# Router rows and logits from one float32 product with unit matrix and gate

## The chip, the cores and the metric

The kernel runs on one core of a Trainium2 chip. The metric is the device time in microseconds of the whole program; the median of several runs counts.

## The reference, cut to what matters

Three layers follow one another on 24576 tokens (8 sequences of 3072) of 256 features. The third routes each token to one of 8 experts:

```
X = rfft(x, axis=1); Y = softshrink(X @ (w_r + i w_i) + b, 0.01); x = irfft(Y)      # per sequence
h = x @ w_in                                                                        # 256 -> 2048
g = where(h >= 1, h, where(h <= -1, 0, (h + 1)**2 / 4));  x = g @ w_out             # 2048 -> 256
logits = x @ w_gate                                                                 # 256 -> 8
expert_idx = argmax(logits);  gate_w = softmax(logits)[expert_idx]
out[mask_e] = gate_w * (relu(x[mask_e] @ w1[e]) @ w2[e])                            # 256 -> 1024 -> 256
```

## The kernel before, in words

It has three stages. `spectral` (to about 560 us in the trace) does the transforms as products of 48 by 64 points; `Moe1` (to about 2927 us) is the dense layer; `Moe2` is the expert layer. The order of all instructions is written out by hand, and each engine and each DMA queue works through its own list in that order.

`Moe1.run` goes through 48 units of 512 tokens, 16 steps each. A step multiplies one slice of 128 hidden features (`layer1`, L664, six products of 512 columns in fp32r, a float32 form that takes one pass and stands as f32 in the products' rows), splits the result of the step before in a high and a low part (ScalarE `gh` L678, GpSimd `gl` L679), multiplies the slice of three steps before into the output bank `po` (`layer2`, L689, six products), and then runs up to three entries of a job list (`router.jobs.run(3)`), at most one of the waiting writes to the slot table (`router.move`, GpSimd's queue), and a piece of the last inverse transform for the next unit (`inv2`, L649, from step 8 of a unit on).

When a unit's output is complete, 18 steps after its first, `Router.add` copies it to `xc` (features on the partitions, two halves of 128, 512 tokens) and puts twelve entries on the job list; `None` is an entry that does nothing:

- `rows(0)`, `rows(1)`: four transposes each (L515) turn two blocks of 128 tokens to rows of 256 features in a bank `prk`, and ScalarE copies the bank to the row tile `rw` (L518).
- `logits`: eight float32 products of 8 columns with the gate `wg` (L524) give the logits of 512 tokens in another bank, and VectorE copies them to a tile `lg` (L526).

After every second unit follows `route`, a generator whose pieces run as further entries: argmax, softmax weight and each token's place in its expert's list on VectorE, a small product (L567), the store of the row tile to the table `xs` in device memory on SP's queue (L574), and eight writes to the slot table on GpSimd's queue (L595). A row of `xs` holds the 256 features, the token's number and its weight. The router's banks come from two buffers, which `inv2` uses too. For 6 steps near the end of the stage the slot writes are held back, while `Moe2` reads the first slots. The jobs of the last unit run inside `Moe2.run`, followed by `list_late`, which makes the list of the remaining expert tiles.

`Moe2` gathers 128 rows of `xs` at a time into `xr` (L913), turns them back to features on the partitions (`turn`, L923), multiplies, and scatters the result.

Of the kernel before, what the change touches and what calls it, by code (L numbers as in the profile page):

```python
# [10 lines left out]
F32 = mybir.dt.float32  # L11
F32R = mybir.dt.float32r
BF16 = mybir.dt.bfloat16
I32 = mybir.dt.int32
U32 = mybir.dt.uint32
AF = mybir.ActivationFunctionType
ALU = mybir.AluOpType
# [5 lines left out]
D = 256  # L23
FF = 2048
NE = 8
# [12 lines left out]
NSMALL = max((NTOK - 512 * NBIG - 129 * m - n) // 256 + m + max(n - NTINY, 0)  # L38
             for m in range(NE + 1) for n in range(NE + 1 - m))
KINDS = {"big": 4, "small": 2, "tiny": 1}  # L40
XW = D + 2
NSLOT = NE * NTOK + 512
NOROW = 65536

# [443 lines left out]
class Router:  # L488


    def __init__(self, tc, nc, a, K, sb, xs_dr, slots):
        self.tc, self.nc, self.K, self.sb, self.xs_dr, self.slots = tc, nc, K, sb, xs_dr, slots
        self.wg = sb.tile([128, 2, NE], F32, name="wg", bufs=1)
        self.open = {}
        self.jobs, self.moves, self.hold = Jobs(), deque(), False
        nc.gpsimd.dma_start(self.wg, a["moe2_w_gate"].rearrange("(c p) e -> p c e", p=128))

    def add(self, u, n, psum):

        sb, nc = self.sb, self.nc  # L500
        k = u % n
        if k == 0:
            self.open[u] = (sb.tile([128, 8, NE], F32, tag="lg", name="lg"),
                            sb.tile([128, 8, XW], F32, tag="rw", name="rw"))
        lg, rw = self.open[u - k]
        xc = sb.tile([128, 2, TT], F32, tag="xc", name="xc")
        nc.scalar.activation(xc, psum, AF.Copy)

        def rows(h):

            p = self.rank_tile()
            for c in range(2):
                for dc in range(2):
                    o = (2 * h + c) * 128
                    nc.tensor.transpose(p[:, (2 * c + dc) * 128:(2 * c + dc + 1) * 128], xc[:, dc, o:o + 128],  # L515
                                        self.K["ident"])
            t = 4 * k + 2 * h
            nc.scalar.activation(rw[:, t:t + 2, 0:D], p.rearrange("p (c d) -> p c d", c=2), AF.Copy)  # L518

        def logits():  # L520
            p = self.rank_tile()
            for c in range(4):
                for dc in range(2):
                    nc.tensor.matmul(p[:, c * NE:(c + 1) * NE], lhsT=xc[:, dc, c * 128:(c + 1) * 128],  # L524
                                     rhs=self.wg[:, dc, :], start=(c == 0 and dc == 0), stop=(c == 3 and dc == 1))
            nc.vector.tensor_copy(out=lg[:, 4 * k:4 * k + 4, :],  # L526
                                  in_=p[:, 0:4 * NE].rearrange("p (c e) -> p c e", c=4))
        self.jobs.add(None, None, None, partial(rows, 0), None, None, partial(rows, 1), None, None, logits, None, None)
        if k == n - 1:
            self.open.pop(u - k)  # L530
            self.jobs.add(self.route(4 * (u - k), 4 * n, lg, rw))

    def route(self, c0, T, lg, rw):
        tc, sb, K = self.tc, self.sb, self.K
        v, sc, pe, gp, sp = self.nc.vector, self.nc.scalar, self.nc.tensor, self.nc.gpsimd, self.nc.sync
        lg, rw = lg[:, 0:T, :], rw[:, 0:T, :]
        sh = [128, T, NE]
        rt, base, ids = K["rt"], K["base"], K["ids"]

        def t3(name, dt=F32):  # L540
            return sb.tile([128, 8 * NE], dt, tag=name, name=name, bufs=1)[:, 0:T * NE]

        def t2(name, dt=F32, bufs=1):
            return sb.tile([128, 8], dt, tag=name, name=name, bufs=bufs)[:, 0:T]

        def by_t(x):
            return x.rearrange("p (e t) -> p t e", t=T)

        mx, r1, sm, si = t2("r_mx"), t2("r_r1"), t2("r_sm"), t2("r_si", I32, 2)
        s1, df, oh, tot = t3("r_s1"), t3("r_df"), t3("r_oh", BF16), t3("r_tot")  # L550
        s1t = s1.rearrange("p (t e) -> p t e", e=NE)
        dft = df.rearrange("p (t e) -> p t e", e=NE)
        mb = mx.unsqueeze(2).to_broadcast(sh)
        v.tensor_reduce(out=mx, in_=lg, axis=AX.X, op=ALU.max)
        v.tensor_tensor(out=s1t, in0=lg, in1=mb, op=ALU.is_equal)
        yield
        v.tensor_tensor(out=s1t, in0=s1t, in1=rt[:, 0:NE].unsqueeze(1).to_broadcast(sh), op=ALU.mult)
        v.tensor_reduce(out=r1, in_=s1t, axis=AX.X, op=ALU.max)
        yield
        v.tensor_tensor(out=by_t(oh), in0=s1t, in1=r1.unsqueeze(2).to_broadcast(sh), op=ALU.is_equal)  # L560
        v.tensor_tensor(out=dft, in0=lg, in1=mb, op=ALU.subtract)
        for _ in range(7):
            yield
        sc.activation(df, df, AF.Exp)
        p = self.rank_tile()[:, 0:2 * T * NE].rearrange("p (i n) -> p i n", i=2)
        for i in range(2):
            pe.matmul(p[:, i, :], lhsT=K["sqb"][:, i, :], rhs=oh, start=True, stop=True)  # L567
        for _ in range(4):
            yield
        v.tensor_reduce(out=sm, in_=dft, axis=AX.X, op=ALU.add)  # L570
        v.tensor_scalar(out=sm, in0=sm, scalar1=1e-9, scalar2=None, op0=ALU.add)
        v.reciprocal(out=rw[:, :, D + 1], in_=sm)
        v.tensor_copy(out=rw[:, :, D].bitcast(I32), in_=ids[:, 0, c0:c0 + T])
        sp.dma_start(self.xs_dr.rearrange("(t p) d -> p t d", p=128)[:, c0:c0 + T, :], rw)  # L574
        yield

        if T == 8:
            v.tensor_tensor_scan(out=tot, data0=rt[:, 2 * NE:2 * NE + T * NE], data1=p[:, 1, :], initial=0.0,
                                 op0=ALU.mult, op1=ALU.add)
        else:  # L580
            for e in range(NE):
                v.tensor_tensor_scan(out=tot[:, e * T:(e + 1) * T], data0=rt[:, 10 * NE:10 * NE + T],
                                     data1=p[:, 1, e * T:(e + 1) * T], initial=0.0, op0=ALU.mult, op1=ALU.add)
        v.tensor_tensor(out=s1, in0=tot, in1=p[:, 0, :], op=ALU.add)
        yield
        s1e = s1.rearrange("p (e t) -> p e t", t=T)
        v.tensor_tensor(out=s1e, in0=s1e, in1=base.unsqueeze(2).to_broadcast([128, NE, T]), op=ALU.add)
        v.tensor_tensor(out=base, in0=base, in1=tot.rearrange("p (e t) -> p e t", t=T)[:, :, T - 1], op=ALU.add)
        yield
        v.tensor_tensor(out=s1, in0=s1, in1=oh, op=ALU.mult)  # L590
        v.tensor_reduce(out=r1, in_=by_t(s1), axis=AX.X, op=ALU.add)
        v.tensor_copy(out=si, in_=r1)

        def place(t):
            apart(tc, gp.indirect_dma_start(  # L595
                out=self.slots, out_offset=bass.IndirectOffsetOnAxis(ap=si[:, t:t + 1], axis=0),
                in_=ids[:, 1, c0 + t:c0 + t + 1], in_offset=None), "slots")
        self.moves.extend(partial(place, t) for t in range(T))
# [121 lines left out]
class Moe2:  # L720
# [197 lines left out]
    def turn(self, t, dc):  # L918
        r, C = self.xr[t], self.chunks(t)
        n = C * 128  # L920
        p = self.ps.tile([128, 512], F32, tag="px", name="px")
        for c in range(C):
            self.nc.tensor.transpose(p[:, c * 128:(c + 1) * 128], r[:, c, dc * 128:(dc + 1) * 128], self.K["ident"])  # L923
        if dc == 0:
            self.xt[t] = (self.sb.tile([128, 2, 512], F32R, tag="xh", name="xh"),
                          self.sb.tile([128, 2, 512], F32R, tag="xl", name="xl"))
        xh, xl = self.xt[t]
        v = self.nc.vector
        self.nc.scalar.activation(xh[:, dc, :n], p[:, :n], AF.Copy)  # L929
        v.tensor_tensor(out=xl[:, dc, :n], in0=p[:, :n], in1=xh[:, dc, :n].bitcast(F32), op=ALU.subtract)  # L930
        if dc == 1:
            o = self.sb.tile([128, 4], I32, tag="oi", name="oi", bufs=4)
            v.tensor_tensor(out=o[:, :C], in0=r[:, :C, D].bitcast(I32), in1=self.ix.pop(t)[2], op=ALU.add)
            self.oi[t] = o

    def layer1(self, t, f):
# [55 lines left out]
    def finish(self, t):  # L992
        tc, nc = self.tc, self.nc
        p, r, o = self.po.pop(t), self.xr.pop(t), self.oi.pop(t)
        C = self.chunks(t)
        y = self.sb.tile([128, 4, D], F32, tag="y", name="y", bufs=3)
        for c in range(C):
            w = r[:, c, D + 1:D + 2]
            if c < C // 2:
                nc.scalar.activation(y[:, c, :], p[:, c, :], AF.Copy, scale=w)  # L1000
            else:
                nc.vector.tensor_scalar(out=y[:, c, :], in0=p[:, c, :], scalar1=w, scalar2=None, op0=ALU.mult)
# [198 lines left out]
```

## Time and profile before

| | |
|---|---|
| median of 3 runs | 4138.6 us (4136.3 to 4139.27) |
| profiled execution | 4134.41 us |
| its span, first to last instruction | 4132.6 us |
| TensorE busy | 4100.5 us, 99% of the span |
| granted TensorE clock, mean | 0.997 |

The profile is of one execution. PE is TensorE's product, PEld its weight load, DVE VectorE, ACT ScalarE, POOL GpSimd, SP the sync engine; L515 is line 515 of the kernel. The durations of TensorE's records overlap, since products are pipelined: what an instruction costs is read from the distance of starts, not from its duration. A releaser behind "<-" is what ended an engine's idle time.

### The profile page before, as it was taken

The numbers are of one execution on the slowest core, as the hardware profiler recorded it, in microseconds if no ns is written. First come the engines' busy times: TensorE is split into PE (matmuls) and PEld (weight loads), VectorE is DVE, ScalarE is ACT, GpSimd is POOL, SyncE is SP. The second block draws the span as 40 slices with busy tenths as digits, with TensorE's granted clock in tenths as the row PEclk, the third lists the DMA queues.
The fourth block names the chain that finished last, engine by engine and source line by source line (L and its number), as shares of the span: only waits on it lengthen the run. The fifth ranks groups of instructions, "written<-read, shape, count | busy, mean of one in ns | idle before, by whom it ended". The sixth has DMA issues, their size and how long they took to land.

```text
span 4132.6 us, 61734 instructions
## 1 busy us (share of the span) xinstructions
PE 4100.5 (99%) x23596; PEld 3564.1 (86%) x23596; DVE 2196.6 (53%) x4082; ACT 1817.9 (44%) x3266; POOL 1794.2 (43%) x1590
## 2 busy tenths in 40 slices
PE   8999999999999999999999999999999999999999
PEld 6999988888888888888888888888889899999998
DVE  6999965555555555555555555555533333333333
ACT  5666544444444444444444444444322322232232
POOL 1000024444445454444454555556455545445453
PEclk9999999999999999999999999999999999999999
DMA  8767512211211221222112210002223321113222
GB/s 263 220 212 215 174 49 48 57 48 45 54 50 50 48 52 47 51 49 49 50 50 56 58 31 22 22 21 62 68 88 108 102 85 46 48 43 130 89 82 74
DMA packets 204344, 321.79 MB, mean 78 GB/s; under 512 B 43284, under 2 KB 167090, under 8 KB 200976
## 3 DMA queue, kind: packets, MB, share of 16 engines
q1 hardware_dynamic: 157968, 213.09, 18.6%
q0 software_dynamic: 46080, 104.76, 8.2%
q8 instruction: 185, 3.03, 0.4%
q14 instruction: 111, 0.91, 0.1%
HBM read 392.10 MB, written 136.61 MB: 128 GB/s over the span
## 4 chain that ended last, share of the span: by engine, by line
PE 97%; DMA 1%; DVE 1%; issue 1%; POOL 0%; ACT 0%; SPq 0%; POOLq 0%; ACTq 0%; DVEq 0%
PE po L689 26%; PE pl L664 26%; PE po L987 13%; PE pl L956 13%; PE pmx L278 6%; PE pi L649 3%; PE pf L225 2%; PE prk L524 2%; PE pf L246 2%; PE pi L305 2%; PE px L923 1%; PE prk L515 1%; DMA A<-ao 1%; DMA xr<-xs,gi 0%; DMA at<-A 0%
## 5 line engine op out<-in xcount | busy, mean ns | idle before, releaser
L679 POOL TENSOR_TENSOR gl<-g,gh 128x512 fp32r<-128x512 f32 x768 | 992.6, 1292 | 1125.4 <-ACT gh L678 1078.9
L670 DVE SCALAR_TENSOR_TENSOR q<-q 128x512 f32<-128x512 f32 x768 | 532.3, 693 | 864.5 <-ACT q L669 862.5
L669 ACT ACTIVATE q<-pl,half 128x512 f32<-128x512 f32 x768 | 527.7, 687 | 1027.8 <-PE pl L664 1027.3
L664 PE MATMUL pl<-yh,win 128*128 128x512 f32 x3072 | 857.8, 401 | 0.9 <-DVE g L671 0.9
L689 PE MATMUL po<-gh,wout 128*128 128x512 f32 x3072 | 835.4, 393 | 0.0
L689 PEld LDWEIGHTS po<-gh,wout 128*128 128x128 f32 x3072 | 576.2, 188 | 125.7
L664 PEld LDWEIGHTS pl<-yh,win 128*128 128x128 f32 x3072 | 556.4, 188 | 113.7 <-DVE g L671 1.8
L961 DVE SCALAR_TENSOR_TENSOR hl<-pl,hh 128x512 fp32r<-128x512 f32 x396 | 273.7, 691 | 576.9 <-ACT hh L960 574.9
L671 DVE TENSOR_TENSOR g<-pl,q 128x512 f32<-128x512 f32 x768 | 531.3, 692 | 83.2 <-DVE q L670 4.6
L960 ACT ACTIVATE hh<-pl 128x512 fp32r<-128x512 f32 x396 | 237.3, 599 | 639.8 <-PE pl L956 625.5
L689 PE MATMUL po<-gl,wout 128*128 128x512 f32 x1536 | 483.6, 395 | 0.0
L678 ACT ACTIVATE gh<-g 128x512 fp32r<-128x512 f32 x768 | 477.2, 621 | 4.2 <-DVE g L671 4.2
L664 PE MATMUL pl<-yl,win 128*128 128x512 f32 x1536 | 474.3, 390 | 0.0
L987 PEld LDWEIGHTS po<-w2b,hh 128*128 128x128 f32 x3232 | 434.9, 188 | 29.1
L956 PE MATMUL pl<-xh,w1b 128*128 128x512 f32 (+1 forms) x1856 | 454.8, 367 | 0.7 <-ACT xh L929 0.7
L987 PE MATMUL po<-w2b,hh 128*128 128x256 f32 x3232 | 449.4, 281 | 0.0
L689 PEld LDWEIGHTS po<-gl,wout 128*128 128x128 f32 x1536 | 288.3, 188 | 69.9
L664 PEld LDWEIGHTS pl<-yl,win 128*128 128x128 f32 x1536 | 288.4, 188 | 65.1
L956 PEld LDWEIGHTS pl<-xh,w1b 128*128 128x128 f32 x1856 | 297.8, 189 | 30.5 <-ACT xh L929 1.3
L1005 POOL DMA_INDIRECT out<-y,oi x202 | 205.2, 1016 | 210.7 <-ACT y L1000 162.7
L956 PE MATMUL pl<-xl,w1b 128*128 128x512 f32 (+1 forms) x928 | 260.0, 361 | 0.0
L987 PE MATMUL po<-w2b,hl 128*128 128x256 f32 x1616 | 258.3, 282 | 0.8 <-DVE hl L961 0.8
(260 smaller groups left out, 4760.1 us busy)
## 6 DMA issues: line engine op xcount, KB each, us to landing
xs<-rw SPq DMA_DIRECT2D x24, 1032.0 KB, 6.5
A<-ao SPq DMA_DIRECT2D x64, 384.0 KB, 4.2
at<-A SPq DMA_DIRECT2D x96, 256.0 KB, 3.7
B<-bo SPq DMA_DIRECT2D x96, 256.0 KB, 2.7
xt<-in_x SPq DMA_DIRECT2D x56, 384.0 KB, 4.8
ws<-in_moe_w SPq DMA_DIRECT2D x128, 128.0 KB, 3.3
w_dr<-wsh SPq DMA_DIRECT2D x128, 128.0 KB, 1.8
w_dr<-wsl SPq DMA_DIRECT2D x128, 128.0 KB, 2.5
```

The costliest lines, as they stand in the source:

```text
L278: pe.matmul(p[:, gi, :], lhsT=l, rhs=r, start=(i == 0), stop=(i == 11))
L664: self.nc.tensor.matmul(p, lhsT=w[:, kc, f * 128:(f + 1) * 128], rhs=y[:, kc, :], start=(i == 0), stop=(i == 5))
L669: self.nc.scalar.activation(q, p, AF.Relu, bias=self.K["half"], scale=0.5)
L670: v.scalar_tensor_tensor(out=q, in0=q, scalar=1.0, in1=q, op0=ALU.min, op1=ALU.mult)
L671: v.tensor_tensor(out=g, in0=p, in1=q, op=ALU.max)
L678: self.nc.scalar.activation(gh, g, AF.Copy)
L679: self.nc.gpsimd.tensor_tensor(out=gl, in0=g, in1=gh.bitcast(F32), op=ALU.subtract)
L689: self.nc.tensor.matmul(self.po[u][:, dc, :], lhsT=w[:, f, dc * 128:(dc + 1) * 128], rhs=g, start=(f == 0 and i == 0), stop=(f == 15 and i ...
L956: self.nc.tensor.matmul(p[:, h * n:(h + 1) * n], lhsT=w[:, part, kc, k * 128:(k + 1) * 128], rhs=x[:, kc, :n], start=(i == 0), stop=(i == 5))
L960: self.nc.scalar.activation(hh, p, AF.Relu)
L961: self.nc.vector.scalar_tensor_tensor(out=hl, in0=p, scalar=0.0, in1=hh.bitcast(F32), op0=ALU.max, op1=ALU.subtract)
L987: self.nc.tensor.matmul(self.po[t][:, c, :], lhsT=h[:, k * n + c * 128:k * n + (c + 1) * 128], rhs=w[:, part, m * f + k, :], start=(first ...
```

## The change

The gate tile `wg` now has 136 columns for each half of the features: for the first half a unit matrix and then the gate's 8 columns, for the second the gate's columns first and then the unit matrix. Four loads on GpSimd's queue fill it. For each block of 128 tokens two float32 products with it write columns 0 to 135 and 128 to 263 of one bank, so that columns 128 to 135 add up to the logits while the others are the features. One ScalarE copy of 264 columns takes all to the row tile. The row is 266 elements wide: 128 features, 8 logits, 128 features, number, weight. `lg` becomes a view of the row tile; the transposes, the separate logits bank and VectorE's copy are gone. A unit now puts 15 entries on the job list, with four groups of products, and the readers in `Moe2` take the new offsets.

```
--- before.py
+++ after.py
@@ -38,7 +38,9 @@
 NSMALL = max((NTOK - 512 * NBIG - 129 * m - n) // 256 + m + max(n - NTINY, 0)
              for m in range(NE + 1) for n in range(NE + 1 - m))
 KINDS = {"big": 4, "small": 2, "tiny": 1}
-XW = D + 2
+
+XL = 128
+XW = D + NE + 2
 NSLOT = NE * NTOK + 512
 NOROW = 65536
 
@@ -490,50 +492,42 @@
 
     def __init__(self, tc, nc, a, K, sb, xs_dr, slots):
         self.tc, self.nc, self.K, self.sb, self.xs_dr, self.slots = tc, nc, K, sb, xs_dr, slots
-        self.wg = sb.tile([128, 2, NE], F32, name="wg", bufs=1)
+
+        self.wg = sb.tile([128, 2, XL + NE], F32, name="wg", bufs=1)
         self.open = {}
         self.jobs, self.moves, self.hold = Jobs(), deque(), False
-        nc.gpsimd.dma_start(self.wg, a["moe2_w_gate"].rearrange("(c p) e -> p c e", p=128))
+        for dc in range(2):
+            nc.gpsimd.dma_start(self.wg[:, dc, dc * NE:dc * NE + 128], a["c_sq"][:, 0, :])
+            nc.gpsimd.dma_start(self.wg[:, dc, XL * (1 - dc):XL * (1 - dc) + NE], a["moe2_w_gate"][dc * 128:(dc + 1) * 128, :])
 
     def add(self, u, n, psum):
 
         sb, nc = self.sb, self.nc
         k = u % n
         if k == 0:
-            self.open[u] = (sb.tile([128, 8, NE], F32, tag="lg", name="lg"),
-                            sb.tile([128, 8, XW], F32, tag="rw", name="rw"))
-        lg, rw = self.open[u - k]
+            self.open[u] = sb.tile([128, 8, XW], F32, tag="rw", name="rw")
+        rw = self.open[u - k]
         xc = sb.tile([128, 2, TT], F32, tag="xc", name="xc")
         nc.scalar.activation(xc, psum, AF.Copy)
 
-        def rows(h):
-
+        def rows(c):
             p = self.rank_tile()
-            for c in range(2):
-                for dc in range(2):
-                    o = (2 * h + c) * 128
-                    nc.tensor.transpose(p[:, (2 * c + dc) * 128:(2 * c + dc + 1) * 128], xc[:, dc, o:o + 128],
-                                        self.K["ident"])
-            t = 4 * k + 2 * h
-            nc.scalar.activation(rw[:, t:t + 2, 0:D], p.rearrange("p (c d) -> p c d", c=2), AF.Copy)
-
-        def logits():
-            p = self.rank_tile()
-            for c in range(4):
-                for dc in range(2):
-                    nc.tensor.matmul(p[:, c * NE:(c + 1) * NE], lhsT=xc[:, dc, c * 128:(c + 1) * 128],
-                                     rhs=self.wg[:, dc, :], start=(c == 0 and dc == 0), stop=(c == 3 and dc == 1))
-            nc.vector.tensor_copy(out=lg[:, 4 * k:4 * k + 4, :],
-                                  in_=p[:, 0:4 * NE].rearrange("p (c e) -> p c e", c=4))
-        self.jobs.add(None, None, None, partial(rows, 0), None, None, partial(rows, 1), None, None, logits, None, None)
+            for dc in range(2):
+                nc.tensor.matmul(p[:, dc * XL:dc * XL + XL + NE], lhsT=xc[:, dc, c * 128:(c + 1) * 128],
+                                 rhs=self.wg[:, dc, :], start=(dc == 0), stop=(dc == 1), skip_group_check=True)
+            nc.scalar.activation(rw[:, 4 * k + c, 0:D + NE], p[:, 0:D + NE], AF.Copy)
+        self.jobs.add(None, None, None)
+        for c in range(4):
+            self.jobs.add(partial(rows, c), None, None)
         if k == n - 1:
             self.open.pop(u - k)
-            self.jobs.add(self.route(4 * (u - k), 4 * n, lg, rw))
-
-    def route(self, c0, T, lg, rw):
+            self.jobs.add(self.route(4 * (u - k), 4 * n, rw))
+
+    def route(self, c0, T, rw):
         tc, sb, K = self.tc, self.sb, self.K
         v, sc, pe, gp, sp = self.nc.vector, self.nc.scalar, self.nc.tensor, self.nc.gpsimd, self.nc.sync
-        lg, rw = lg[:, 0:T, :], rw[:, 0:T, :]
+        rw = rw[:, 0:T, :]
+        lg = rw[:, :, XL:XL + NE]
         sh = [128, T, NE]
         rt, base, ids = K["rt"], K["base"], K["ids"]
 
@@ -569,8 +563,8 @@
             yield
         v.tensor_reduce(out=sm, in_=dft, axis=AX.X, op=ALU.add)
         v.tensor_scalar(out=sm, in0=sm, scalar1=1e-9, scalar2=None, op0=ALU.add)
-        v.reciprocal(out=rw[:, :, D + 1], in_=sm)
-        v.tensor_copy(out=rw[:, :, D].bitcast(I32), in_=ids[:, 0, c0:c0 + T])
+        v.reciprocal(out=rw[:, :, XW - 1], in_=sm)
+        v.tensor_copy(out=rw[:, :, XW - 2].bitcast(I32), in_=ids[:, 0, c0:c0 + T])
         sp.dma_start(self.xs_dr.rearrange("(t p) d -> p t d", p=128)[:, c0:c0 + T, :], rw)
         yield
 
@@ -920,7 +914,7 @@
         n = C * 128
         p = self.ps.tile([128, 512], F32, tag="px", name="px")
         for c in range(C):
-            self.nc.tensor.transpose(p[:, c * 128:(c + 1) * 128], r[:, c, dc * 128:(dc + 1) * 128], self.K["ident"])
+            self.nc.tensor.transpose(p[:, c * 128:(c + 1) * 128], r[:, c, dc * (XL + NE):dc * (XL + NE) + 128], self.K["ident"])
         if dc == 0:
             self.xt[t] = (self.sb.tile([128, 2, 512], F32R, tag="xh", name="xh"),
                           self.sb.tile([128, 2, 512], F32R, tag="xl", name="xl"))
@@ -930,7 +924,7 @@
         v.tensor_tensor(out=xl[:, dc, :n], in0=p[:, :n], in1=xh[:, dc, :n].bitcast(F32), op=ALU.subtract)
         if dc == 1:
             o = self.sb.tile([128, 4], I32, tag="oi", name="oi", bufs=4)
-            v.tensor_tensor(out=o[:, :C], in0=r[:, :C, D].bitcast(I32), in1=self.ix.pop(t)[2], op=ALU.add)
+            v.tensor_tensor(out=o[:, :C], in0=r[:, :C, XW - 2].bitcast(I32), in1=self.ix.pop(t)[2], op=ALU.add)
             self.oi[t] = o
 
     def layer1(self, t, f):
@@ -995,7 +989,7 @@
         C = self.chunks(t)
         y = self.sb.tile([128, 4, D], F32, tag="y", name="y", bufs=3)
         for c in range(C):
-            w = r[:, c, D + 1:D + 2]
+            w = r[:, c, XW - 1:XW]
             if c < C // 2:
                 nc.scalar.activation(y[:, c, :], p[:, c, :], AF.Copy, scale=w)
             else:
```

## Rows read from the trace of the kernel before

**Rows 1.** The page: engines' busy us, share, instructions; busy tenths and clock in 40 slices
```profile
PE 4100.5 (99%) x23596; PEld 3564.1 (86%) x23596; DVE 2196.6 (53%) x4082; ACT 1817.9 (44%) x3266; POOL 1794.2 (43%) x1590
...
PEclk9999999999999999999999999999999999999999
```

**Rows 2.** The page: the chain of waits that ended last, by engine and by line
```profile
PE 97%; DMA 1%; DVE 1%; issue 1%; POOL 0%; ACT 0%; SPq 0%; POOLq 0%; ACTq 0%; DVEq 0%
PE po L689 26%; PE pl L664 26%; PE po L987 13%; PE pl L956 13%; PE pmx L278 6%; PE pi L649 3%; PE pf L225 2%; PE prk L524 2%; PE pf L246 2%; PE pi L305 2%; PE px L923 1%; PE prk L515 1%; DMA A<-ao 1%; DMA xr<-xs,gi 0%; DMA at<-A 0%
```

**Rows 3.** Busy time of each engine by stretch: the dense stage
```profile
core 0: us, PE busy (x) PEld busy (x) DVE busy (x) ACT busy (x) POOL busy (x), PEclk, DMA share, GB/s
...
560.00:2927.00 2367.00, 2366.09 (x11367) 1958.68 (x11366) 1292.41 (x2313) 1139.42 (x2011) 1188.20 (x966) 1.00 0.18 45
```

**Rows 4.** TensorE's waits, 560 to 2927 us: total us, times, longest
```profile
PE pl L664 <- DVE g L671: 0.9, 1, 0.9
```

**Rows 5.** TensorE in order of time, first unit: start us, us, what (merged)
```profile
605.59 1.08 PE L664 MATMUL pl<-yh,win 128*128 128x512 f32 x4
...
608.35 1.08 PE L664 MATMUL pl<-yh,win 128*128 128x512 f32 x4
...
611.12 0.60 PE L515 MATMUL prk<-ident,xc 128*128 128x128 f32 x4
611.48 1.17 PE L664 MATMUL pl<-yh,win 128*128 128x512 f32 x4
...
614.68 1.17 PE L664 MATMUL pl<-yh,win 128*128 128x512 f32 x4
...
617.53 1.85 PE L524 MATMUL prk<-wg,xc 128*128 128x8 f32 x16
619.23 1.17 PE L664 MATMUL pl<-yh,win 128*128 128x512 f32 x4
...
622.09 1.08 PE L664 MATMUL pl<-yh,win 128*128 128x512 f32 x4
```

**Rows 6.** Busy time by stretch: one unit's router steps, and five quiet steps
```profile
608.35:622.09 13.74, 13.74 (x73) 11.58 (x72) 5.73 (x10) 7.06 (x12) 5.14 (x4) 1.00 0.01 1
580.68:594.52 13.84, 13.84 (x62) 11.26 (x60) 6.92 (x11) 6.04 (x11) 6.47 (x5) 1.00 0.01 2
```

**Rows 7.** The tile prk: records, ns min/median/max, first and last start, forms
```profile
L524 PEld LDWEIGHTS prk<-wg,xc x768: 187/192/192, 617.3 to 2938.6; 128*128 128x128 f32 x192
L524 PE MATMUL prk<-wg,xc x768: 170/256/256, 617.5 to 2938.6; 128*128 128x8 f32 x192
L515 PEld LDWEIGHTS prk<-ident,xc x384: 138/141/142, 610.9 to 2934.0; 128*128 128x128 f32 x192
L515 PE MATMUL prk<-ident,xc x384: 270/272/273, 611.1 to 2934.1; 128*128 128x128 f32 x192
L518 ACT ACTIVATE rw<-prk x96: 595/601/603, 611.8 to 2934.4; 128x512 f32<-128x512 f32 x96
L526 DVE COPY lg<-prk x48: 190/192/192, 619.4 to 2938.9; 128x32 f32<-128x32 f32 x48
```

**Rows 8.** TensorE in order of time, first stage (L246: float32, 128 columns)
```profile
399.80 0.64 PE L278 MATMUL pmx<-wh,xh 128*128 128x256 f32 x4
...
402.63 0.28 PE L305 MATMUL pi<-zh,i1h 128*128 128x256 f32 x1
...
403.34 1.05 PE L246 MATMUL pf<-f,at 128*128 128x128 f32 x8
404.15 0.72 PE L278 MATMUL pmx<-wh,xh 128*128 128x256 f32 x4
```

**Rows 9.** Lines L278 and L664, fp32r products of 256 and 512 columns
```profile
L278 PE MATMUL pmx<-wh,xh x12: 278/281/364, 399.8 to 404.6; 128*128 128x256 f32 x12
...
L664 PE MATMUL pl<-yh,win x3072: 387/393/504, 558.7 to 2920.7; 128*128 128x512 f32 x192
```

**Rows 10.** Groups by form: busy us, mean ns, idle before
```profile
L254 ACT ACTIVATE xh<-pf 128x256 fp32r<-128x256 f32 x88 | 33.5, 381 | 0.0
```

**Rows 11.** ScalarE in order of time, first unit
```profile
611.76 0.60 ACT L518 ACTIVATE rw<-prk 128x512 f32<-128x512 f32 x1 [0.63 <-PE prk L515]
613.15 0.69 ACT L669 ACTIVATE q<-pl,half 128x512 f32<-128x512 f32 x1 [0.78 <-PE pl L664]
```

**Rows 12.** GpSimd in order of time, where the second stage begins
```profile
550.86 0.75 POOL L496 DMA_DIRECT2D wg<-in_moe_w_gate  x1 [48.11 <-DVE vv L282]
563.28 1.28 POOL L679 TENSOR_TENSOR gl<-g,gh 128x512 fp32r<-128x512 f32 x1 [11.68 <-ACT gh L678]
```

**Rows 13.** DMA issues: queue, count, KB each, us to landing
```profile
xs<-rw SPq DMA_DIRECT2D x24, 1032.0 KB, 6.5
```

## The prediction

> **What bounds the kernel now.** I read the page first: TensorE is busy 99% of the span, no other engine over 53%, and the granted clock is in its top tenth in every slice [rows 1]. The chain of waits that ended last confirms it: 97% of the span is TensorE work, of which the router's two product lines L524 and L515 have 2% and 1% [rows 2]. The kernel therefore gets shorter only by what leaves TensorE's queue, or longer by what enters it or by a wait that it has not got now. The change acts in the second stage, the dense layer, from about 560 to 2927 us. There TensorE is busy 2366.09 of 2367.00 us at a granted clock of 1.00, the upper level of 2.4 GHz; ScalarE, VectorE and GpSimd are each busy about half of it [rows 3]. The waits of TensorE in that stage come to one row of 0.9 us [rows 4]. So each router instruction on TensorE is paid in full, and its price can be read as the delay that it causes to the dense layer's products behind it.
>
> **What the router costs now, on TensorE.** A step of the stage starts with the L664 products. A step without router work takes 608.35 - 605.59 = 2.76 us. Of one unit's router steps the starts stand at 608.35, 611.48, 614.68, 619.23 and 622.09 [rows 5]: 13.74 us for four steps, where four quiet ones take 4 x 2.765 = 11.06 (the five quiet steps of another stretch take 13.84 us [rows 6]: 2.77 each, so 11.07). The unit's router work costs 13.74 - 11.07 = 2.67 us. It splits as the rows do. The step from 611.48 to 614.68 has one group of four transposes and takes 3.20, so 0.43 us for four, 0.108 each. The step with the logits takes 4.55, so 1.78 us for 16 records, 0.111 each. The logits are 8 products (4 blocks by 2 halves) and 16 records, since each float32 product runs as two passes with a weight load each, whereas a transpose is one record: 768 against 384 [rows 7]. The sum 8 x 0.108 + 16 x 0.111 = 2.64 us agrees with 2.67.
>
> **What the change puts in its place.** Per unit 4 blocks x 2 halves = 8 float32 products of 128x128 weights with 136 columns, so 16 passes. The weight loads are those of the logits before (the same xc slices); the eight transposes go, and each pass streams 136 columns where it streamed 8. All hangs on the price of a pass with 136 columns, which no row of before shows. The bounds:
>
> - From below: 8 columns cost 0.111 us a pass. The float32 products of the first stage have 128 columns [rows 8]: eight passes start at 403.34, the next products at 404.15, and these take 0.72 where an undisturbed group takes 0.64, so (0.81 + 0.08) / 8 = 0.111 us a pass. From 8 to 128 columns the price does not move: the weight load sets it, and the columns hide behind it. 136 columns can't be under 0.111.
> - From above: a float32 column seems to take the array twice as long as one of the fp32r products. The shortest records are 170 ns for 8 columns and 270 for 128 [rows 7], (270 - 170) / 120 = 0.83 ns a column; the fp32r products go from 281 ns at 256 columns to 393 at 512 [rows 9], 0.44 ns a column. So 136 float32 columns are like 272 of those. The fp32r groups with 256 columns go from 399.80 to 402.63 for 24 passes [rows 8], 0.118 each, and 0.118 x 272 / 256 = 0.125.
> - Between them: the transposes load their weights in 141 ns where the products take 192 [rows 7], and still cost 0.108 at 128 columns, or within a group (0.60 - 0.27) / 3 = 0.11 [rows 5, 7]; 0.109 in the middle. I read that as the streaming of 128 float32 columns. At 136 it is 0.109 x 136 / 128 = 0.116, just above what the weight load asks. I take 0.116, nearer to the lower end because the row at 128 columns already sits there.
>
> So 16 x 0.116 = 1.86 us a unit, against 2.67: 0.81 us less, and over 48 units 39 us less. With 0.111 it is 0.89 x 48 = 43 us, with 0.125 it is 0.67 x 48 = 32 us.
>
> The Trainium skill speaks against this edit: "TensorE: Matmul & The Clock Gate", Terms, the row on the xbus, says that the load and the product gained a transpose mode that is four times as fast for float32. By that rule a product with a unit matrix would cost four transposes. The trace has a ratio of two at 128 columns (2 x 0.111 against 0.109), so it does not agree here; the rule would give the first rival's time.
>
> **The other edits, each at nothing, and their cover.**
> - Copies out of the bank. ScalarE had two of 128x512 at 601 ns a unit and VectorE one of 192 ns [rows 7]; ScalarE now has four of 128x264. The nearest row is 128x256 at 381 ns [rows 10], so about 390 each, 1.56 us instead of 1.20. ScalarE's own timeline has the cover: the copy at 611.76 ends at 612.36, and the next activation, for which it waits 0.78 us, starts at 613.15 [rows 11]. The shorter copy ends earlier. Behind it queue the activation q and, through it, the dense layer's VectorE work; neither moves.
> - Banks. One router tile is taken per step, as before, from two buffers shared with L649. A tile's copy ends 1.2 us after its group starts (611.12 to 612.36 [rows 5, 11]), and the tile is asked for again two steps, over 5 us, later. The four groups instead of three fill steps 3 to 6 of the unit instead of 3 to 5; the pieces of L649 begin at step 8 of its unit, so they still don't meet.
> - One step later for the route: 15 entries of the job list instead of 12 at 3 a step. Its VectorE work, the store xs on SP's queue, its small product and its eight slot writes on GpSimd move by one step, 2.77 us. The expert lists follow. One of the eight slot writes of units 42 and 43 falls into the steps in which such writes are held and comes 6 steps later, behind the four slot reads on GpSimd's queue; only GpSimd waits for those. The first tile of the late list is asked for more than ten steps after the list is ready, so no TensorE work waits for it.
> - Three more loads on GpSimd's queue for the gate tile, at 0.75 us each 2.25. GpSimd has 11.68 us idle between this load and its first gl [rows 12]. If that cover were gone, TensorE would wait once, by at most that 2.25 us.
> - The row is 1064 bytes instead of 1032, in stores that land in 6.5 us [rows 13], 3% more; the gathers take the same number of rows. All are far ahead of their readers.
>
> At the seams between the stages the tiles stand at new addresses, which may move a wait by 1 or 2 us either way.
>
> **Sum.** The profiled execution took 4134.4 us (span 4132.6 and 1.8 around it): 4134.4 - 39 = 4095.4. The median of the runs shown is 4138.6, 4.2 us above it; carried over, 4099.6. I say 4099.
>
> **Rivals.**
> 1. Slower: the 136 columns are not hidden. If a product cost four transposes (above), it would be 4 x 0.109 x 136 / 128 = 0.463 us, eight of them 3.71 us a unit against 2.67, 1.04 x 48 = 50 us: 4189. The same side is reached if a product over 128 columns were cut in two pieces with weight loads of their own: 32 x 0.111 = 3.55 us, 42 us slower, 4181. It decides at 2.67 / 16 = 0.167 us a pass. Against it: 256 fp32r columns take 0.118, and 128 float32 columns are entirely under the weight load [rows 8]. 6%.
> 2. The time comes back as a wait: TensorE no longer fills the step and waits for a copy or for gl, so that the steps keep their length. For it: ScalarE holds one more copy a unit. Against it: quiet steps of 2.77 us run with no wait, so the other engines keep up with a step that has no router work at all. If every group had to wait for its copy (0.39 us, and four a unit), it would take back 1.56 x 48 = 75 us: 4174; to take back just the gain, 0.2 us a group. Time near 4139: 5%.
> 3. A smaller gain: the pass costs over 0.125 (0.14: 2.24 us, 21 us gained, 4118), or the first expert tiles lose some us on GpSimd's queue, where slot writes stand ahead of gathers. 4110 to 4130: 9%.
>
> **How the numbers follow.** Forecast (0.111 to 0.125 a pass, 43 to 32 us gained, 4096 to 4107): 80%. A measurement of this kernel can tell about 0.2%, 8 us, from no change. Faster by more: the forecast and rival 3, 89%; within: 5%; slower: 6%. The range takes the forecast's bounds, 4 us below for the seams and 5 above: 4092 to 4112, some 84%.
>
> **What would show it.** Right: the router's products are 768 records of 136 columns at one line, no transposes at L515; the unit's five steps exceed five quiet ones by 1.8 to 2.0 us; TensorE's busy time falls by 32 to 43 us and its waits in the stage stay under 2 us; the records and gaps outside the router stay. Wrong: passes over 0.13 us apart; a row of waits of the router's product on the copy; a gap at the start of the expert stage behind a gather.

## The result, and the profile after

The changed kernel takes 4072.25 us (median of 4 runs, 4071.59 to 4077.35), the kernel before 4137.45 in the same comparison: a ratio of 0.9846, 95% interval 0.9829 to 0.9864. It gained 65 us where the forecast was 39, and lies below the stated range. The profiled execution took 4072.76 us with a span of 4071.0, 61.6 us under the span of before; the account below is made in spans.

The page of the changed kernel, engines and the chain of waits by line, against [rows 1, 2]:

```profile
PE 4039.8 (99%) x23212; PEld 3531.0 (87%) x23212; DVE 2223.9 (55%) x4034; ACT 1836.2 (45%) x3362; POOL 1836.2 (45%) x1593
...
PE pl L658 26%; PE po L683 26%; PE po L981 14%; PE pl L950 13%; PE pmx L280 5%; PE pi L643 3%; PE prk L516 2%; PE pf L227 2%; PE pf L248 2%; PE pi L307 1%; PE px L917 1%; DMA at<-A 1%; DMA A<-ao 1%; DVE zl L298 0%; DVE vv L284 0%
```

TensorE is still the bound. Its busy time fell by 60.7 us, as much as the span, and it has 384 records fewer: the transposes. (L658 and L683 are the lines that were L664 and L689; L516 is the new router product.)

The tile prk of the changed kernel, against [rows 7]: records, ns min/median/max, first and last start, forms.

```profile
L516 PEld LDWEIGHTS prk<-wg,xc x768: 187/189/190, 613.2 to 2881.7; 128*128 128x128 f32 x192
L516 PE MATMUL prk<-wg,xc x768: 277/279/279, 613.4 to 2881.8; 128*128 128x136 f32 x192
L518 ACT ACTIVATE rw<-prk x192: 387/393/396, 614.1 to 2882.1; 128x264 f32<-128x264 f32 x192
```

The router has the 768 passes that were forecast, and the copy takes the 390 ns. TensorE's timeline of the changed kernel, two quiet steps and the first unit, against [rows 5]:

```profile
605.22 1.07 PE L658 MATMUL pl<-yh,win 128*128 128x512 f32 x4
...
607.94 1.07 PE L658 MATMUL pl<-yh,win 128*128 128x512 f32 x4
...
610.66 1.07 PE L658 MATMUL pl<-yh,win 128*128 128x512 f32 x4
...
613.39 0.63 PE L516 MATMUL prk<-wg,xc 128*128 128x136 f32 x4
613.77 1.18 PE L658 MATMUL pl<-yh,win 128*128 128x512 f32 x4
...
617.01 1.18 PE L658 MATMUL pl<-yh,win 128*128 128x512 f32 x4
...
626.34 1.07 PE L658 MATMUL pl<-yh,win 128*128 128x512 f32 x4
```

Two things are to be seen. A group of four passes takes 0.63 us to the end of the last, whose own duration is 0.28, so (0.63 - 0.28) / 3 = 0.117 us a pass: the forecast's 0.116 stands. But a quiet step, without any router work, now takes 607.94 - 605.22 = 2.72 us where it took 2.76 to 2.77 [rows 5, 6], and its group of four dense products 1.07 instead of 1.08. Nothing in the change touches a quiet step's instructions. The distances between the starts of successive records say more than the merged lines; their medians over all quiet steps that follow a quiet one, in ns, first the six products on yh and yl, then the six on gh and gl:

```
before (345 steps): 232 233 231 227 227 227 | 234 224 237 229 238 229   sum 2767
after  (298 steps): 227 227 227 227 227 227 | 227 227 227 227 227 227   sum 2720 (with the fractions)
```

Over the dense stage as a whole, the first and last start of the first-layer product, against its row in [rows 9]:

```profile
L658 PE MATMUL pl<-yh,win x3072: 387/389/628, 560.2 to 2862.0; 128*128 128x512 f32 x192
```

2301.8 us where it was 2362.0: 60.2 of the 61.6 us are there. TensorE's waits in the stage did not grow; its one row there is:

```profile
PE pl L658 <- DVE g L665: 0.9, 3, 0.6
```

### The profile page after: what moved, and what is told of

It is laid out like the page before. It is cut to its first block, busy times and chain, and to the rows that moved or that the text cites. A ratio compares the mean times of both kernels' runs of the same rounds, so it can differ in the third digit from the quotient of the medians.

```text
span 4071.0 us, 61018 instructions
## 1 busy us (share of the span) xinstructions
PE 4039.8 (99%) x23212; PEld 3531.0 (87%) x23212; DVE 2223.9 (55%) x4034; ACT 1836.2 (45%) x3362; POOL 1836.2 (45%) x1593
## 4 chain that ended last, share of the span: by engine, by line
PE 94%; DVE 3%; DMA 1%; issue 1%; ACT 1%; POOL 0%; SPq 0%; DVEq 0%; POOLq 0%; ACTq 0%
PE pl L658 26%; PE po L683 26%; PE po L981 14%; PE pl L950 13%; PE pmx L280 5%; PE pi L643 3%; PE prk L516 2%; PE pf L227 2%; PE pf L248 2%; PE pi L307 1%; PE px L917 1%; DMA at<-A 1%; DMA A<-ao 1%; DVE zl L298 0%; DVE vv L284 0%
## 5 line engine op out<-in xcount | busy, mean ns | idle before, releaser
L664 DVE SCALAR_TENSOR_TENSOR q<-q 128x512 f32<-128x512 f32 x768 | 545.4, 710 | 823.4 <-ACT q L663 821.6
L658 PE MATMUL pl<-yh,win 128*128 128x512 f32 x3072 | 858.9, 401 | 1.0 <-DVE g L665 0.9
L683 PE MATMUL po<-gh,wout 128*128 128x512 f32 x3072 | 825.4, 390 | 0.0
L683 PEld LDWEIGHTS po<-gh,wout 128*128 128x128 f32 x3072 | 576.8, 188 | 123.5
L658 PEld LDWEIGHTS pl<-yh,win 128*128 128x128 f32 x3072 | 553.4, 189 | 99.5 <-DVE g L665 3.1
L658 PE MATMUL pl<-yl,win 128*128 128x512 f32 x1536 | 474.5, 390 | 0.0
L683 PE MATMUL po<-gl,wout 128*128 128x512 f32 x1536 | 474.2, 390 | 0.0
L981 PEld LDWEIGHTS po<-w2b,hh 128*128 128x128 f32 x3232 | 433.4, 188 | 29.8
L658 PEld LDWEIGHTS pl<-yl,win 128*128 128x128 f32 x1536 | 288.6, 188 | 64.8
L683 PEld LDWEIGHTS po<-gl,wout 128*128 128x128 f32 x1536 | 288.3, 188 | 62.0 <-POOL gl L673 0.2
```

The source lines that it names most:

```text
L658: self.nc.tensor.matmul(p, lhsT=w[:, kc, f * 128:(f + 1) * 128], rhs=y[:, kc, :], start=(i == 0), stop=(i == 5))
L664: v.scalar_tensor_tensor(out=q, in0=q, scalar=1.0, in1=q, op0=ALU.min, op1=ALU.mult)
L683: self.nc.tensor.matmul(self.po[u][:, dc, :], lhsT=w[:, f, dc * 128:(dc + 1) * 128], rhs=g, start=(f == 0 and i == 0), stop=(f == 15 and i ...
L981: self.nc.tensor.matmul(self.po[t][:, c, :], lhsT=h[:, k * n + c * 128:k * n + (c + 1) * 128], rhs=w[:, part, m * f + k, :], start=(first ...
```

## What could make untouched products faster

**Theory A, addresses.** The gate tile and the rows grew, the logits tile went, and together they push the dense stage's work tiles q, g, gh, gl up by 1408 bytes in each partition (gl, for example, from byte 110944 to 112352; addresses here and below are those of the built programs). All else that a quiet step reads, the weights win and wout and the operands yh and yl, stands where it stood. Theory A is that the place of these tiles sets the pace. **Rival B** is that the shorter router work leaves TensorE's stream in a better state, which then lasts through the quiet steps. Four kernels tell them apart. They, and four of the runs further on, ran on chips on which the kernel before takes some 4280 us, with long gaps in the expert stage of every kernel that was traced there; so ratios to it, steps and lengths of the dense stage are compared, not times.

**The kernel before with the tiles moved alone.**

```
 cb = P.open("c_b", bufs=2)
+cb.tile([128, 352], F32, name="pad", bufs=1)
```

> The kernel before with 1408 unused bytes a partition ahead of the dense stage's work tiles q, g, gh, gl, which puts these at the addresses that they have after the change; nothing else differs. Theory A (where these tiles lie sets the distance of the 512-column products, 227 ns after and about 231 before): a quiet step falls from 2.77 to 2.72 us and the time by 20 to 30 us, to about 4110. Rival B (the shorter router work itself leaves the stream of products in a better state): quiet steps stay at 2.77 us, time stays near 4137.

The ratio is 0.9934 (0.9918 to 0.9951). TensorE's timeline of this kernel, quiet steps, and the row of the first-layer product:

```profile
586.23 1.07 PE L664 MATMUL pl<-yh,win 128*128 128x512 f32 x4
...
588.95 1.07 PE L664 MATMUL pl<-yh,win 128*128 128x512 f32 x4
```

```profile
L664 PE MATMUL pl<-yh,win x3072: 387/389/628, 561.0 to 2893.2; 128*128 128x512 f32 x192
```

A quiet step takes 2.72 us, and the dense stage 2332.2 us, 29.8 under that of before, with the router of before. Theory A holds; rival B has no place left for the quiet steps.

**The changed kernel with the tiles put back.** One xc buffer frees 4096 bytes, a pad of 2688 leaves q, g, gh, gl at the addresses of before.

```
-xc = sb.tile([128, 2, TT], F32, tag="xc", name="xc")
+xc = sb.tile([128, 2, TT], F32, tag="xc", name="xc", bufs=1)
 cb = P.open("c_b", bufs=2)
+cb.tile([128, 672], F32, name="pad", bufs=1)
```

> The changed kernel with q, g, gh, gl back at the addresses of before (one xc buffer instead of two, and 2688 unused bytes). Theory A: quiet steps go back to 2.77 us and the time to 4137 - 38 = about 4099, which is the forecast. Rival B: quiet steps stay at 2.72, time stays at 4072.

The ratio is 0.9931 (0.9915 to 0.9948). TensorE's timeline of this kernel, a quiet step and the first unit:

```profile
608.72 1.08 PE L658 MATMUL pl<-yh,win 128*128 128x512 f32 x4
...
611.48 1.08 PE L658 MATMUL pl<-yh,win 128*128 128x512 f32 x4
...
614.25 0.62 PE L516 MATMUL prk<-wg,xc 128*128 128x136 f32 x4
614.62 1.18 PE L658 MATMUL pl<-yh,win 128*128 128x512 f32 x4
...
627.17 1.07 PE L658 MATMUL pl<-yh,win 128*128 128x512 f32 x4
```

```profile
L658 PE MATMUL pl<-yh,win x3072: 387/393/574, 561.7 to 2885.0; 128*128 128x512 f32 x192
```

Quiet steps are back at 2.76. The unit's five steps take 627.17 - 611.48 = 15.69 us, 1.85 more than five quiet ones of 2.767; the forecast was 1.86. The stage lasts 2323.3 us, 38.7 less than before; the forecast was 39. In the dense stage this is the change as it was predicted, without the move that came with it.

**Control: one xc buffer, tiles not put back.** As the last kernel, with a pad of 4096 bytes.

> Control for the run with the addresses of before: the changed kernel with one xc buffer, and 4096 unused bytes that keep q, g, gh, gl where they are after the change. If the second xc buffer hides nothing, both theories expect 4072 within 4 us and quiet steps of 2.72. If it was needed, TensorE waits for xc at the first router product of each unit and the time is longer.

The ratio is 0.9879 (0.9862 to 0.9896), and the stage is that of the changed kernel, 2302.9 us:

```profile
L658 PE MATMUL pl<-yh,win x3072: 387/389/628, 563.0 to 2865.9; 128*128 128x512 f32 x192
```

So the single buffer costs nothing in the stage, and the 20.4 us between this kernel and the last are due to the addresses. The whole times of these two fell less than their expectations say: about 4099 and 4072 us would be ratios of 0.991 and 0.984, just outside the intervals. The gaps of the expert stage lie in these times too, and the changed kernel itself was not run on that chip, so the account holds for the dense stage alone.

**Which of the four tiles.** In the kernel before, the pad stands between g and gh:

```
 g = self.sb.tile([128, TT], F32, tag="g", name="g")
+if (u, f) == (0, 1):
+    self.sb.tile([128, 352], F32, name="pad", bufs=1)
```

> The kernel before with the 1408 bytes between g and gh, so that gh and gl (the operands of the second layer's products) move and q and g stay. Theory A1 (the address of TensorE's own moving operand counts): time near 4110 as with all four moved, with the gain at the second layer's products. Theory A2 (the address of what ScalarE, VectorE and GpSimd read and write beside the products, q and g, counts): little of the gain, time near 4137. Rival B: 4137.

The ratio is 0.9947 (0.993 to 0.9963), the stage 2333.1 us, as with all four moved:

```profile
L664 PE MATMUL pl<-yh,win x3072: 387/389/628, 562.6 to 2895.7; 128*128 128x512 f32 x192
```

It is A1: what TensorE itself reads. All twelve products of a quiet step go to 227 ns, so the first layer's first three, whose operands never moved, were slow only behind slow ones. With the pad between gh and gl, gl alone moves:

```
+if (u, f) == (0, 0):
+    self.sb.tile([128, 352], F32, name="pad", bufs=1)
 gl = self.sb.tile([128, TT], F32R, tag="gl", name="gl", bufs=4)
```

> The kernel before with 1408 unused bytes between gh and gl, so that gl alone (the low parts, written by GpSimd and read by the last two products of a step) moves. If each operand's own address counts, the four products on gh keep their 234, 224, 237 and 229 ns and only those on gl get to 227: a quiet step near 2.75 us. If the address at which GpSimd writes counts, all six get to 227 and the step takes 2.72; if gh's address alone counts, the step stays at 2.77.

TensorE's timeline of this kernel, one quiet step (L691 is the second layer):

```profile
652.14 1.07 PE L664 MATMUL pl<-yh,win 128*128 128x512 f32 x4
653.05 0.62 PE L664 MATMUL pl<-yl,win 128*128 128x512 f32 x2
653.50 1.09 PE L691 MATMUL po<-gh,wout 128*128 128x512 f32 x4
654.43 0.63 PE L691 MATMUL po<-gl,wout 128*128 128x512 f32 x2
654.89 1.07 PE L664 MATMUL pl<-yh,win 128*128 128x512 f32 x4
```

The step takes 2.75 us, as was expected if each operand's own address counts, but the gain is not where it was expected. By the medians of the distances, the four products on gh keep 234, 224, 237 and 229 ns. The two on gl go from 238 and 229 to 232 and 233, together only 2 ns less, not to 227. The first layer's first three, behind them, go from 232, 233 and 231 to 231, 227 and 227. So what gl's new place does is to let the stream find its pace sooner; that each product's own address sets its own distance is not shown.

## Which address is good

Two sweeps move gh and gl within the changed kernel, one by 128 bytes every three units, the other by 32 bytes every unit (one buffer of xc and rw, three of gh and gl, of twice the size). These sweeps, those further on and the run with gl alone are one run each; a quiet step has the same median in every run and on every chip where the places are the same (2.767 us at 96 and 2.720 at 224, with the weights, yh and yl at 224). The edit of the second sweep, cut to gh:

```
-gh = self.sb.tile([128, TT], F32R, tag="gh", name="gh", bufs=4)
+gh = self.sb.tile([128, 2 * TT], F32R, tag="gh", name="gh", bufs=3)[:, 8 * u:8 * u + TT]
```

> The changed kernel with gh and gl in buffers of twice the size, in which every three units use a place 128 bytes further on: 16 places over 2048 bytes, the first (place 0) at the address of before modulo 2048, place 11 at that of after. xc and rw have one buffer, gh and gl three. If the place of gh and gl inside a power of two sets the pace, quiet steps of place 0 take 2.77 us and those of place 11 take 2.72, and the others show the period and which places are fast. If something else that moved along counts (the tiles' distance from each other, or what lay under them), quiet steps have one length over all places.

> As the sweep by 128 bytes, but each unit 32 bytes further on, over 1536 bytes from the address of before. If the pace changes in blocks of 128 bytes or more, neighbouring units have the same quiet steps, with edges between; if alignment to 64 bytes counts, even and odd units differ; both theories of the first sweep hold here too.

In the first, quiet steps take 2.767 us at the eight even places and 2.720 at the eight odd ones, so the period is 256 bytes or a part of it. In the second, TensorE's timeline where unit 3 (192 modulo 256) and unit 4 (224) are multiplied:

```profile
748.00 1.09 PE L658 MATMUL pl<-yh,win 128*128 128x512 f32 x4
...
749.39 1.10 PE L683 MATMUL po<-gh,wout 128*128 128x512 f32 x4
...
750.79 1.09 PE L658 MATMUL pl<-yh,win 128*128 128x512 f32 x4
...
796.37 1.07 PE L658 MATMUL pl<-yh,win 128*128 128x512 f32 x4
...
797.73 1.07 PE L683 MATMUL po<-gh,wout 128*128 128x512 f32 x4
...
799.09 1.07 PE L658 MATMUL pl<-yh,win 128*128 128x512 f32 x4
```

A quiet step takes 2.79 us at 192 and 2.72 at 224. One place in eight is good, and it comes back every 256 bytes. It is 224, and 224 is also where the weights, yh and yl stand. Two more sweeps by 32 bytes ask which of these it must agree with, or whether 224 is good as such. In the one yh and yl stand 64 bytes lower, at 160; in the other the weights do too:

```
 wp = P.open("wp", bufs=1, side="right")
+wp.tile([128, 16], F32, name="pad_w")     # below the weights; in the other kernel above them
```

> The sweep of gh and gl by 32 bytes, with yh and yl (the first layer's moving operands) 64 bytes lower, at 160 modulo 256; the weights win and wout stay at 224. Theory P (a product keeps its pace where its moving operand and its weights stand at one address modulo 256): no place gives the quiet step of 2.72 us, since the six first-layer products are off by themselves; at 224 the six second-layer products alone are near 227 ns. Theory M (successive moving operands must agree): 2.72 us at place 160. Theory Z (224 as such is the good address): as P here.

> The same sweep with weights, yh and yl all 64 bytes lower, at 160 modulo 256. Theory P (operand and weights agree modulo 256): 2.72 us at place 160 and not at 224. Theory Z (224 as such): no place has 2.72, and 224 is best for the second-layer products.

TensorE's timeline with yh and yl alone at 160, unit 2 (gh and gl at 160):

```profile
697.12 1.09 PE L658 MATMUL pl<-yh,win 128*128 128x512 f32 x4
...
699.91 1.09 PE L658 MATMUL pl<-yh,win 128*128 128x512 f32 x4
```

And with the weights at 160 as well, unit 2 (160) and unit 4 (224):

```profile
697.75 1.07 PE L658 MATMUL pl<-yh,win 128*128 128x512 f32 x4
...
700.47 1.07 PE L658 MATMUL pl<-yh,win 128*128 128x512 f32 x4
...
791.99 1.09 PE L658 MATMUL pl<-yh,win 128*128 128x512 f32 x4
...
794.77 1.09 PE L658 MATMUL pl<-yh,win 128*128 128x512 f32 x4
```

All quiet steps that follow a quiet one in the three sweeps by 32 bytes, worked out from the starts of the first-layer products (medians, us):

```
gh, gl modulo 256:              96     128    160    192    224    0      32     64
weights, yh, yl at 224          2.767  2.778  2.780  2.787  2.720  2.787  2.773  2.793
weights, yh, yl at 160          2.780  2.787  2.720  2.787  2.773  2.793  2.767  2.789
weights at 224, yh, yl at 160   2.793  2.806  2.800  2.780  2.780  2.780  2.767  2.807
```

The good place moved with the weights and yh together, from 224 to 160: 224 as such is not it, and theory Z falls. Where gh agrees with yh but not with the weights (last row, 160), the step is 2.80, among the slowest: theory M falls. At place 160 the second and the third row differ in the address of the weights alone, 2.72 us against 2.80. Theory P stands for the step as a whole: it takes 2.72 us where all its moving operands and weights agree modulo 256, and at no other place of the sweeps. It is not a law for each product by itself: in the last row at 224 the second layer agrees with its weights, and its six distances are 226, 236, 229, 232, 231 and 227, still uneven behind six products that disagree, where near 227 was expected. And since all weights of the stage stand at one address modulo 256, the runs don't tell whether a product's own weights count or those that are loaded for the next while it runs.

## Is a kernel with all operands aligned faster still?

The changed kernel with everything that TensorE reads in the dense and expert stages at 224 modulo 256 (order of the constants, a gate tile of two halves of 768 bytes, five pads, one buffer of xc; the edit in short):

```
-self.wg = sb.tile([128, 2, XL + NE], F32, name="wg", bufs=1)
+self.wg = sb.tile([128, 2, 192], F32, name="wg", bufs=1)[:, :, 0:XL + NE]
+pre.tile([128, 24], F32, name="pad_pre"); rp.tile([128, 32], F32, name="pad_rp", bufs=1)
+cb.tile([128, 24], F32, name="pad", bufs=1); ds.tile([128, 24], F32, name="pad_d", bufs=1)
+self.sb.tile([128, 32], F32, name="pad_o", bufs=1)     # behind oi, ahead of hh and hl
```

> The changed kernel with all that TensorE reads in the dense and the expert stage at 224 modulo 256: gate tile (its halves 768 bytes apart), xc, unit matrix, the inverse transform's table, both expert weights' buffers, xh, xl, hh, hl; xc has one buffer. Theory P: the dense stage keeps quiet steps of 2.72 us, the steps with a router group get shorter than 3.24 us, and a large expert step falls from 2.82 to 2.72-2.75 us, which over some 300 such steps of work is 20 to 35 us: a ratio to the run of the changed kernel beside it of about 0.993. If address agreement counts for long fp32r products alone, the expert stage changes little and the ratio is 0.998 to 1.0.

> The changed kernel itself, on the chip of these runs, as the measure for the aligned one: all theories expect 0.984 to 0.989 of the kernel before and the stage lengths of its first profile (dense stage 2298 us).

These two ran on one chip, on which the kernel before takes 4137.51 us. The changed kernel has 4074.18 us, 0.9848 (0.9831 to 0.9864); the aligned one 4077.55, 0.9857 (0.9841 to 0.9873): no gain. The dense stage got 1.3 us shorter (2300.1 against 2301.4, first to last start as above; the 2298 in the expectation should have been 2301.8). The expert stage did not. A large step there, of a tile of 512 tokens, has six products of 512 columns and then twelve of 256 (aligned, the twelve, up to the next step):

```profile
2991.58 1.12 PE L983 MATMUL po<-w2b,hh 128*128 128x256 f32 x8
...
2993.01 1.09 PE L952 MATMUL pl<-xh,w1b 128*128 128x512 f32 x4
```

And the changed kernel beside it:

```profile
2991.85 1.09 PE L981 MATMUL po<-w2b,hh 128*128 128x256 f32 x8
...
2993.25 1.08 PE L950 MATMUL pl<-xh,w1b 128*128 128x512 f32 x4
...
2994.63 1.11 PE L981 MATMUL po<-w2b,hh 128*128 128x256 f32 x8
...
2996.05 1.09 PE L950 MATMUL pl<-xh,w1b 128*128 128x512 f32 x4
...
2997.44 1.11 PE L981 MATMUL po<-w2b,hh 128*128 128x256 f32 x8
...
2998.87 0.40 PE L950 MATMUL pl<-xh,w1b 128*128 128x512 f32 x1
```

The twelve take 1.43 us aligned, and 1.40, 1.42 and 1.43 not aligned. Over all large tiles of the two traces, from the starts of the records, the mean is 1.43 us aligned and 1.42 not aligned: 1.40 where the second layer's weights stand at 128 and 1.43 to 1.44 where they stand at 224, both with hh at 96. The six products of 512 columns take 1.38 us in the changed kernel where xh and the weights agree and 1.39 to 1.41 where they don't, as theory P has it, and 1.39 in the aligned one. A whole large step is 2.80 to 2.83 us in the changed kernel and 2.82 aligned, where 2.72 to 2.75 was expected. A last run moved hh and hl by 32 bytes every two expert tiles:

```
-hh = self.sb.tile([128, 512], F32R, tag="hh", name="hh", bufs=3)
+hh = self.sb.tile([128, 640], F32R, tag="hh", name="hh", bufs=3)[:, 8 * (t // 2 % 8):8 * (t // 2 % 8) + 512]
```

> The changed kernel with hh and hl of the expert stage 32 bytes further on every two tiles, over the 256 bytes from 96 modulo 256; the second layer's weights stand at 128 in every other large tile and at 224 in the rest. Theory P as it stands for 512 columns would give the shortest products of 256 columns where hh and weights agree modulo 256 (place 1 for the weights at 128, place 4 for those at 224). The aligned run speaks against that: agreement gave a steady 120 ns, and disagreement 115 to 122. Then the shortest lie at another place, near 117 on average, and the best place would be worth some 0.03 us a step against agreement.

In these products the roles are turned: TensorE loads slices of hh or hl, and the weights w2b stream past. Mean distances of successive products in the large tiles, in ns, from the starts of the records (groups slowed by the gaps left out; "-" no large tile at that place):

```
hh, hl modulo 256:    96     128    160    192    224    0      32     64
weights at 128        116.7  119.2  118.3  114.6  118.4  -      119.8  117.8
weights at 224        119.4  119.8  116.6  116.9  -      118.2  117.0  -
```

The addresses count here too, but agreement is among the slow places (119.2 at 128 under weights at 128; 119.5 at 224 under 224, in the aligned kernel, since no large tile of the sweep had it); the 114.6 rests on one tile. What the rule is for 256 columns stays open, and no version better than the changed kernel was found.

## Why the prediction was wrong

- **The product swap was right, in mechanism and size.** A pass of 136 columns costs 0.116 us as taken, two passes a product, no new wait. At the addresses of before the unit costs 1.85 us (forecast 1.86) and the stage 38.7 us less (forecast 39).
- **What failed is the cover of one edit.** The prediction put the larger gate tile and row under edits at nothing, and said of new addresses only that they "may move a wait by 1 or 2 us either way" at the seams, and under what would show it that "the records and gaps outside the router stay". They did not stay: the move of gh and gl by 1408 bytes, from 96 to 224 modulo 256, took 47 ns from each quiet step. Alone it is worth 29.8 us in the stage of the kernel before. On top of the swap it is worth 2323.3 - 2301.8 = 21.5 (20.4 against the control), so the stage's 60.2 are the 38.7 of the swap and this. It is worth less there because the stream loses its pace behind each router group, and there are now four a unit: the 188 steps that hold one such group take 602.9 us in sum with the tiles put back and 602.6 in the changed kernel, so nearly all of the 21.5 lies in the other steps. Nothing in the change aimed at this third of the gain; that the new place was the good one of eight is luck.
- **In the changed kernel itself** the router costs 626.34 - 610.66 - 5 x 2.72 = 2.08 us a unit against its own quiet steps, 0.22 more than forecast. That is not the passes but the products behind them: after a group the next ten or so run at 224 to 236 ns before they are at 227 again (median distances 318, 235, 233, 236, 224, 231, 236, 228, 232, 231, 227).
- **Rivals.** None of them shows in the runs: a float32 product of 136 columns costs two passes of 0.116 us, not four transposes, and its 768 records say that it was not cut. The waits of TensorE stayed at 0.9 us. The copies, the later route, the held slot write and GpSimd's four loads (0.53 to 0.58 us each, done at 551.86) cost nothing that a trace shows.

## What to carry to other kernels

When an edit changes the size of any tile, compare the addresses of all that the bounding engine reads, before and after; a gain or loss outside the edited code is then the first thing to look for, and a pad in the kernel before tests it in one run. Read the distances of record starts in steps that the edit does not touch, before crediting the edit. Where a forecast rests on "nothing else moves", give the layout a bound of its own: here it was 47 ns on a 2.77 us step, 1.7%.

## What the runs showed of the hardware that was not expected

- In the dense stage, at a granted clock of 1.00 (2.4 GHz), a stream of products of 512 fp32r columns runs at 227 ns a product where all moving operands and weights stand at one address modulo 256 bytes, and at 224 to 240 where they do not, over a whole step 1.7 to 3.2% slower (2.767 to 2.807 against 2.720). The Trainium skill, "TensorE: Matmul & The Clock Gate", section "Part 2: What happens when you issue a matmul", gives the streaming operand and the weight load read ports of their own, so that the one takes no bandwidth from the other; the runs show a pace that depends on the two addresses together. Why it does was not settled.
- Past a disturbance the stream finds back to 227 ns after three products (behind a second layer whose operands disagree, in the kernel before) to eleven (behind a router group), and was seen to do so only where its operands agree.
- A float32 pass costs the same at 8 columns and at 128 (0.112 us, L524 and L246 of the kernel before), so columns don't set it there, and 0.116 at 136. The transposes' 0.108 for 128 columns, scaled to 136, is an estimate of 0.115, so there the columns may.
